# One core, attention beside a gated MLP: first-chunk key copies on ScalarE's queue, weight loads issued in unit 32, Wo's rows at unit 25

## The chip, the cores and the metric

The kernel runs on one core of a Trainium2 chip. A core has a matrix engine (TensorE, PE in the profile; its weight loads are PEld), VectorE (DVE), ScalarE (ACT), GpSimd (POOL) and SyncE (SP), which here only issues DMAs. Each engine takes its own instructions in program order and meets the others through semaphores. DMAs are issued from SyncE's and ScalarE's instruction queues and are carried out by 16 DMA engines. The metric is device time in microseconds (us) of one execution.

## What is computed

One transformer block on 2048 tokens of width 576: attention with 32 heads of 18 and a sliding window of 256, and a gated MLP of width 4608, both on the same normalised input.

```python
def reference(A_x, A_wqkv, A_wo, B_x, B_w1, B_w3, B_w2):
    # H = 32; Dh = 18; W = 256
    xn = _layernorm(A_x)
    q, k, v = split_heads(xn @ A_wqkv)
    scores = einsum("bhqd,bhkd->bhqk", q, k) * Dh ** -0.5
    mask = (i - j >= 0) & (i - j < W)
    p = softmax(where(mask, scores, -1e9))
    attn = merge_heads(p @ v) @ A_wo
    mlp = (silu(xn @ B_w1) * (xn @ B_w3)) @ B_w2
    return A_x + attn + mlp
```

## The kernel before

The program is one instruction stream for each engine, written out by Python: `add(engine, fn, r=..., w=..., j=...)` appends an instruction and notes which buffers it reads, writes or joins in writing, and the needed semaphore waits follow from that. The place of the `add` call in the Python program is the place on the engine.

The tokens are worked in four chunks `c` of 512. In a chunk, TensorE goes through 36 **units** `u` (`NF`): unit `u` makes 128 rows of the MLP's hidden layer, 9 pairs `n` of matmuls each (line 860), half of them on `xnT` (the normalised input, transposed) and half on `xnS` (the same with its two halves of partitions swapped by DMA). A unit's result goes through `unit_tanh` on ScalarE (L869) and `unit_h` on VectorE (L875, L878). Three pairs of PSUM banks take turns. Between the pairs of matmuls stand the score matmuls of attention (L682; their exponential on ScalarE is L691, masks on GpSimd L718), and now and then a block of P·V (L739). At the end of a chunk come the projections of the next chunk's Q, K and V (L496) and then the second MLP matmul with Wo (`w2_lanes`: L1036, L1045, with a part of the next chunk's scores, L756).

Four things in it are touched by the change:

- **The MLP's first weights.** A tile `w13` holds the weights of four units (fc 0 to 8 of a chunk). `load_part` (L343) issues the next part of the next tile from SyncE. Parts are `owed`: the counter is raised after certain units, and after pairs 3 and 8 of each unit `owe_part(op)` issues one, behind that matmul. The two parts of the next chunk's first tile (fc 9 counted through) were issued at the start of the projections, after `xn_swap` (L460).
- **The first chunk's last keys.** `kn` holds keys in a second layout for the groups `g` 0 to 3; its first 256 columns (`knp`) are, for chunk 1, the last 256 keys of chunk 0. `first_prev(only)` (L653) copies them out of `stage` in eight DMAs: three of 18 partitions x 4 groups x 256, three of 18 x 256 and two of 9 x 256. They were issued from SyncE in units 18 to 25, one in each. `kn` is cleared by GpSimd ahead of them, at unit 15 (L1480).
- **Wo's first rows.** Four DMAs (L1477) load `wo[0:126]` from SyncE; the rest (`wo_late`) follows in the projections. `wo` is first read in `w2_lanes` of chunk 0.
- **What stands near them on SyncE**: the transposes of the next chunk's input (`xnT<-xn`, L453), the attention outputs' moves (`oT<-od`, L817), the loads of `w2` (L379), in program order.

Of the kernel before, what the change touches and what calls it, by code (L numbers as in the profile page):

```python
# [44 lines left out]
class _Prog:  # L45
# [13 lines left out]
    def add(self, eng, fn, r=(), w=(), j=(), dma=None, after=()):  # L59
        deps = []  # L60
        for k in r:
            deps += self.bufs[k].writers
        for k in w:
            g = self.bufs.get(k)
            if g is not None:
                deps += g.ahead(eng)
        for k in j:
            g = self.bufs[k].before
            if g is not None:
                deps += g.ahead(eng)  # L70
        op = _Op(eng, fn, deps + list(after), dma)
        op.after = tuple(after)
        self.n[eng] += 1
        op.pos = self.n[eng]
        if dma is not None:
            self.dma_count[dma] = self.dma_count.get(dma, 0) + 16
            op.cnt = self.dma_count[dma]
        for k in r:
            self.bufs[k].readers.append(op)
        for k in w:  # L80
            self.bufs[k] = _Gen([op], self.bufs.get(k))
        for k in j:
            self.bufs[k].writers.append(op)
        for k in w:
            if self.bufs[k].before is not None:
                self.bufs[k].before.before = None
        self.ops.append(op)
        return op
# [76 lines left out]
def bass_parallel_sum__sliding_block__glu_gated_swiglu__prompt_kernel(  # L165
# [18 lines left out]
    NC = S // CH  # L184
# [11 lines left out]
    add = P.add  # L196

    with ExitStack() as es:
# [65 lines left out]
        def st_keys(*tiles):  # L264
            return [("sh", t) for t in tiles]
# [27 lines left out]
        def job():  # L293
            nonlocal job_ctr
            i = job_ctr % 3
            job_ctr += 1
            return JOBS[i]
# [24 lines left out]
        def w13_at(k):  # L322
            if k == 3:
                return NW13, hT[:, 18:27, :]
            s = (k if k < 3 else k - 1) % NW13
            return s, w13[s]

        owed = 0
# [4 lines left out]
        def load_part(after=(), behind=(), eng="sp"):  # L333
            nonlocal nfill
            if nfill >= len(parts_of):
                return
            k, n, a, b = parts_of[nfill]
            first = a == 0 and n == 0
            s, dst = w13_at(k)
            c0 = (k % NFC) * 512  # L340
            src = (B_w3, B_w1)[n]
            nfill += 1
            add(eng, lambda e: e.dma_start(  # L343
                dst[64 * n:64 * n + 64, a:b, :],
                src[64 * a:64 * b, c0:c0 + 512].rearrange("(kd p) f -> p kd f", p=64)),
                r=list(behind), after=after, dma=f"w13_{s}_{n}", **{"w" if first else "j": [("w13", s)]})
# [182 lines left out]
        def proj_end(later=None):  # L529
            if pend:  # L530
                c, what, banks, last = pend.pop()
                proj_part(c, what, banks, 1, last)
                proj_out(c, what, banks, later)
                return what
# [106 lines left out]
        def last_keys(g, to, of):  # L641
            if g != SPREAD:
                r0 = (g - (g > SPREAD)) * Dh
                return [(kn[96:96 + Dh, g, to], stage[r0:r0 + Dh, 8, of], [8])]
            return [(kn[96 + r:96 + r + 2 * 9 - 1:2, g, to], stage[126 + r:127 + r, :, of], range(9)) for r in range(2)]

        def first_prev(only):
            moves = [(kn[32 * h:32 * h + Dh, :, 0:W], stage[(4 + h) * Dh:(5 + h) * Dh, 0:GN, CH - W:CH], range(GN)) for h in range(3)]
            for g in range(GN):
                moves += last_keys(g, slice(0, W), slice(CH - W, CH))  # L650
            for n, (dst, src, tset) in enumerate(moves):
                if n in only:
                    add("sp", lambda e, dst=dst, src=src: e.dma_start(dst, src), r=st_keys(*tset), dma="knp",  # L653
                        **{"j" if n else "w": [("knp", g) for g in range(GN)]})

        def keep_new(g):
# [4 lines left out]
        def keep_keys(g):  # L661
            add("pool", lambda e: e.tensor_copy(
                kb4[:, g - GN, :, :].bitcast(dt.float32), kv[:, g, 2 * NB - NV:NB, :].bitcast(dt.float32)),
                r=[("k", g)], w=[("kp", g)])
# [485 lines left out]
        for p in range(2):  # L1150
            add("act", lambda e, p=p: e.dma_start(
                wvr[64 * p:64 * p + 64, :], A_wqkv[512:576, 2 * D + p * HD:2 * D + (p + 1) * HD]),
                dma="wvd", **{"j" if p else "w": ["wvd"]})
# [11 lines left out]
        for h in range(2):  # L1165
            for n in range(2):
# [3 lines left out]
                    dma=f"wqk{h}", **{"j" if n else "w": [f"wqk{h}"]})  # L1170
# [33 lines left out]
        def turn(i):  # L1204
# [6 lines left out]
            r=[("sm", 2), "eps"], w=[("sm", 3)])  # L1211
# [23 lines left out]
        for h in range(2):  # L1235
# [13 lines left out]
            for k0, k1, need, key, which in parts:  # L1249
                for n, (dst, src) in enumerate(moves[m] for m in which):  # L1250
                    dealt.append(add("pool", lambda e, dst=dst[:, k0:k1], src=src[:, k0:k1]: e.tensor_copy(dst, src),
                                     r=need + ([] if dealt else [("xnd", 1)]), **{"j" if n else "w": [key]}))
# [45 lines left out]
        for c in range(NC):  # L1298
# [93 lines left out]
            for u in range(NF):  # L1392
# [77 lines left out]
                    span_last(2, G, slice(0, 1))  # L1470
                if c == 0 and u in (5, 6):
                    span_last(2, G, (slice(1, 3), slice(3, None))[u - 5])
                if c == 0 and u == 13:
                    for t in range(4):
                        a0 = (4 + 14 * (t // 2)) * Dh
                        rows = A_wo[a0:a0 + 14 * Dh, :].rearrange("(s p d) f -> p s d f", p=2, d=Dh)[t % 2, :, :, :]
                        add("sp", lambda e, t=t, rows=rows: e.dma_start(wo[0:126, t, :], rows),  # L1477
                            dma="wo", **{"j" if t else "w": ["wo"]})
                if c == 0 and u == 15:
                    add("pool", lambda e: e.memset(kn[:, :, :].bitcast(dt.float32), 0.0),  # L1480
                        w=[(k, g) for k in ("kn", "knp") for g in range(GN)])
                if c == 0 and u == 20:
                    add("dve", lambda e: e.memset(wz[:], 0.0), w=["wz"])
                if c == 0 and 18 <= u < 26:
                    first_prev((u - 18,))
                if u in (range(27, 31) if c == 0 else range(LATE_PV + 5, LATE_PV + 12, 2)):
                    load_w2(c * 2 * NFC + 4)
                if u == 29 and c + 1 == NC:
# [3 lines left out]
            if c + 1 < NC:  # L1492
                banks = job()
                pv(c, 3, banks)
                for g in range(GN, G):
                    keep_keys(g)
                if c == 0:
                    add("pool", lambda e: e.memset(mk16[:, :, :], -1.0), w=["mkn"] + [("k", g) for g in range(GN)])
                    add("pool", lambda e: e.affine_select(
                        out=mk16[:, 0, :], in_=mk16[:, 0, :], compare_op=ALU.is_ge, fill=0.0,  # L1500
                        base=-1, pattern=[[-1, 128]], channel_multiplier=1), r=["mkn"], w=["mkn"])
                    add("pool", lambda e: e.affine_select(
                        out=mk16[:, 1, :], in_=mk16[:, 1, :], compare_op=ALU.is_ge, fill=0.0,
                        base=0, pattern=[[1, 128]], channel_multiplier=-1), r=["mkn"], w=["mkn"])
                    v0_readers = {p: list(P.bufs[("va", p)].readers) for p in range(NB)}
                for m, what in enumerate(PROJ_LATER + [None]):
                    got = proj_begin(c + 1, what) if what else proj_end()
                    if m == 0:
                        xn_swap(c + 1, ("sp", "sp"))
                        for _ in range(2):  # L1510
                            load_part()
                        if c == 0:
                            wo_late()
                        for u in sorted(side):
                            for do in side.pop(u):
                                do()
                        pv_out(banks[0], 0)
                        pv_out(banks[1], 1)
                        o_scale(0)
                    elif m == 1:  # L1520
                        o_turn(6, 0)
                        o_turn(6, 1)
                        o_scale(1)
                    elif m == 2:
                        o_turn(7, 0)
                        o_turn(7, 1)
                    if got == ("q", 2):
                        new_k(0)
                        new_k(1)
                    elif got and got[0] == "8":  # L1530
                        new_k(2)
                    if m == 6:
                        o_pack(3, "sp")
                    if 3 <= m < 7:
                        new_q(m - 3, "act")
                    owe_part(last_pe())
                i_last = (job_ctr - 1) % 3
                live = [*SC, *JOBS[(i_last + 1) % 3]]
                late_pv = w2_lanes(c, live, [*JOBS[(i_last - 1) % 3], *JOBS[i_last]])
                continue  # L1540
# [52 lines left out]
```

## Time and profile before

| | |
|---|---|
| median of 3 runs | 555.41 us (555.14 to 555.68) |
| profiled execution | 555.78 us, of which the span of instructions is 554.0 |
| TensorE clock granted | 1.00 throughout |
| TensorE busy | 548.4 us, 99% |
| VectorE, ScalarE, GpSimd busy | 66%, 53%, 22% |
| DMA | 88.12 MB, 159 GB/s on average |

A row of the profile's groups and timelines gives the line of the program, the engine, the operation, what it writes and reads (`out<-in`) and a count; a timeline row begins with the start and the duration in us, and ends with the idle time before it and what ended that. ACTq and SPq are the instruction queues of ScalarE and SyncE, in which DMA issues stand. Times are from the start of the span. The chain of work that ended last is TensorE for 96% of the span. In chunk 0 the units run from 21.1 to 103 us, in chunks 1 to 3 from 163 to 239, 299 to 375 and 434 to 510.

### The profile page before, as it was taken

To read this page: it belongs to the slowest core of one execution; us is meant where nothing else is said; L and a number is where in the kernel's file an instruction comes from. 1 tells how busy PE (TensorE), PEld (TensorE's weight loads), DVE (VectorE), ACT (ScalarE), POOL (GpSimd) and SP (SyncE) were. 2 spreads that over 40 slices of the span, in tenths; PEclk is the share of its full clock that TensorE was granted. 3 is DMA by queue.
4 is the path that set the end of the run, shared out by engine and by line. 5 is a ranking of instruction groups with operands and counts; after the bars stand their busy time and mean duration, and the time that the engine had idled before them with its cause. 6 is when DMAs were issued, how large, how long until landed. Compare 5 with 4: busy or idle time off the path is not lost.

```text
span 554.0 us, 17657 instructions
## 1 busy us (share of the span) xinstructions
PE 548.4 (99%) x7690; PEld 301.9 (54%) x7690; DVE 365.0 (66%) x745; ACT 294.0 (53%) x481; POOL 120.1 (22%) x281
## 2 busy tenths in 40 slices
PE   8999999999999999999999999999999999999998
PEld 4455444465564444456556445446555644545776
DVE  6566898845748888674664888866466686676211
ACT  6457775268735554526882655443787355554000
POOL 5413653300003332210001342320000222221000
DMA  9997989549999998965979999767697999881552
GB/s 243 208 193 141 205 159 183 137 97 176 156 163 202 187 197 134 155 130 116 155 136 190 197 198 189 147 101 156 120 160 125 196 196 165 168 167 61 139 151 64
DMA packets 166070, 88.12 MB, mean 159 GB/s; under 512 B 101546, under 2 KB 163754, under 8 KB 165994
## 3 DMA queue, kind: packets, MB, share of 16 engines
q1 hardware_dynamic: 164874, 85.42, 82.3%
q10 hardware_dynamic: 1120, 1.59, 1.0%
q8 instruction: 60, 0.98, 0.8%
q14 instruction: 16, 0.13, 0.1%
HBM read 71.30 MB, written 2.36 MB: 133 GB/s over the span
## 4 chain that ended last, share of the span: by engine, by line
PE 96%; DMA 2%; SPq 1%; issue 0%; ACT 0%; DVE 0%
PE ps L860 50%; PE ps L1036 17%; PE ps L496 7%; PE ps L932 6%; PE ps L682 4%; PE ps L1086 2%; PE ps L739 2%; PE ps L1045 2%; DMA xnS<-xnT 2%; PE ps L791 2%; PE ps L756 1%; PE ps L1160 1%; PE ps L939 1%; SPq L343 1%; PE ps L1096 0%
## 5 line engine op out<-in xcount | busy, mean ns | idle before, releaser
L860 PE MATMUL ps<-xnT,w 64*128 64x512 bf16 x1400 | 177.5, 376 | 0.8 <-issue 0.8
L860 PE MATMUL ps<-xnS,w 64*128 64x512 bf16 x1120 | 148.6, 376 | 0.7 <-DMA xnS<-xnT 0.7
L875 DVE SCALAR_TENSOR_TENSOR gs<-thb,ps 128x512 bf16<-128x512 bf16 x144 | 98.6, 684 | 67.2 <-ACT thb L869 66.7
L869 ACT ACTIVATE thb<-ps 128x512 bf16<-128x512 f32 x144 | 85.7, 595 | 59.8 <-PE ps L860 58.6
L1036 PE MATMUL ps<-hT,w 32*128 32x512 bf16 x1728 | 107.0, 374 | 0.0
L860 PEld LDWEIGHTS ps<-xnT,w 64*128 64x128 bf16 x1400 | 67.2, 94 | 72.5 <-issue 1.0
L878 DVE SCALAR_TENSOR_TENSOR hT<-gs,ps 128x512 bf16<-128x512 bf16 x144 | 98.9, 687 | 5.0
L860 PEld LDWEIGHTS ps<-xnS,w 64*128 64x128 bf16 x1120 | 53.7, 94 | 58.1 <-DMA xnS<-xnT 1.1
L1036 PEld LDWEIGHTS ps<-hT,w 32*128 32x128 bf16 x1728 | 57.5, 92 | 30.2 <-issue 1.4
L763 ACT ACTIVATE pt<-ps 128x512 bf16<-128x512 f32 x120 | 65.1, 595 | 7.7 <-PE ps L756 7.5
L691 ACT ACTIVATE pt<-ps 128x1024 bf16<-128x1024 f32 (+1 forms) x46 | 46.2, 1004 | 43.0 <-PE ps L682 42.9
L756 PE MATMUL ps<-qv,kn 18*128 18x384 bf16 (+2 forms) x288 | 54.5, 267 | 0.0
L806 POOL TENSOR_TENSOR oq<-uq,rden 128x288 bf16<-128x288 f32 x15 | 10.1, 673 | 198.6 <-DVE rden L805 198.6
L718 POOL TENSOR_TENSOR pt<-pt,mk 128x128 int32<-128x128 int32 (+1 forms) x82 | 33.1, 424 | 69.4 <-ACT pt L691 69.4
L771 DVE TENSOR_TENSOR pt<-pt,kv 128x256 int32<-128x256 int32 x96 | 31.4, 371 | 24.8 <-ACT pt L763 24.2
L496 PE MATMUL ps<-xnT,wp 64*128 64x512 bf16 (+1 forms) x360 | 38.0, 355 | 0.0
L932 PE MATMUL ps<-w,hT 128*128 128x288 bf16 (+1 forms) x292 | 36.9, 284 | 0.0
L691 ACT ACTIVATE hT<-ps 128x1024 bf16<-128x1024 f32 (+1 forms) x20 | 20.0, 1002 | 31.5 <-PE ps L682 31.4
L756 PEld LDWEIGHTS ps<-qv,kn 18*128 18x128 bf16 x288 | 26.5, 93 | 13.8 <-DVE uq L800 0.8
L932 PEld LDWEIGHTS ps<-w,hT 128*128 128x128 bf16 x292 | 28.2, 98 | 7.3 <-issue 0.2
L682 PE MATMUL ps<-qv,kv 64*128 64x320 bf16 (+4 forms) x336 | 31.7, 258 | 0.0
L813 DVE STREAM_TRANSPOSE od<-oq 128x256 bf16<-128x256 bf16 x64 | 25.1, 424 | 6.3 <-POOL oq L806 6.3
(128 smaller groups left out, 523.4 us busy)
## 6 DMA issues: line engine op xcount, KB each, us to landing
w<-in_B_w_dram SPq DMA_DIRECT2D x60, 576.0 KB, 7.8
w<-in_B_w_dram SPq DMA_DIRECT2D x72, 288.0 KB, 4.4
w<-in_B_w_dram SPq DMA_DIRECT2D x12, 192.0 KB, 6.8
xp<-in_A_x_dram SPq DMA_DIRECT2D x4, 576.0 KB, 5.4
xnS<-xnT SPq DMA_DIRECT2D x8, 256.0 KB, 4.4
xp<-in_A_x_dram SPq DMA_DIRECT2D x14, 144.0 KB, 4.2
w<-in_B_w_dram SPq DMA_DIRECT2D x6, 320.0 KB, 4.8
oT<-od SPq DMA_DIRECT2D x52, 36.0 KB
```

Of the source, the lines that this page charges most:

```text
L496: op = add("pe", lambda e, out_=out_, st=st, mv=mv, n=n, r0=r0, first=first: e.matmul(out_, st, mv, start=first, stop=(part == 1 and n == ...
L682: add("pe", lambda e, r0=r0, out_=out_, kb=kb, q0=q0, nb=nb: e.matmul(out_, kb4[r0:r0 + 64, g - GN, kb + NV - NB, :] if kb < 0 else kv[r0: ...
L691: add("act", lambda e: e.activation(pt_slot(sl)[:, 0:w, :], PS[:, SC[0]:SC[1] + 1, 0:w].rearrange("p r q -> p q r"), ACT.Exp, scale=scale) ...
L718: add("pool", lambda e, vb=vb, mm=mm: e.tensor_tensor(vb, vb, mm, ALU.mult), r=(key if n == 0 else []) + ["mk"], **{"w" if n == 0 else "j" ...
L756: add("pe", lambda e: e.matmul(PS[:, b, c0:c0 + nb * 128], kn[32 * a:32 * a + Dh, g, W + 128 * jb:W + 128 * jb + 128], qv[32 * a:32 * a + ...
L763: add("act", lambda e: e.activation(head_of(sl, p), PS[:, b, :], ACT.Exp, scale=scale), r=[("ps", b)], **{"j" if p else "w": pt_keys(sl)})
L860: op = add("pe", lambda e, n=n, r0=r0, r=r, k=k, src=src: e.matmul(PS[:, b0 + r, :], wt[r0:r0 + 64, k, fl * 128:(fl + 1) * 128], src, star ...
L869: add("act", lambda e: e.activation(th[i][:], PS[:, bg, :], ACT.Tanh, scale=0.5), r=[("ps", bg)], w=[("th", i)])
L875: add("dve", lambda e: e.scalar_tensor_tensor(out=gs[i][:], in0=th[i][:], scalar=1.0, in1=PS[:, bg, :], op0=ALU.add, op1=ALU.mult), r=[("t ...
L878: add("dve", lambda e: e.scalar_tensor_tensor(out=hT[:, u, :], in0=gs[i][:], scalar=0.5, in1=PS[:, bu, :], op0=ALU.mult, op1=ALU.mult), r= ...
L932: add("pe", lambda e: e.matmul(bank, hT[:, f, tt * 128:(tt + 1) * 128], w2[sl][:, k, n0:n1], start=first, stop=(c + 1 == NC and half == 1 ...
L1036: add("pe", lambda e, b=b, rows=rows, wt=wt, fl=fl, k=k, a=a, first=first: e.matmul(PS[:, b, :], wt[rows, fl, :], hT[rows, k, :], start=fi ...
```

## The change

The key copies are issued by ScalarE, two after each of units 1 to 4, and the clearing of `kn` moves to unit 0. Wo's first rows are issued at unit 25 instead of 13. Two more parts are owed after unit 31 in chunks 0 to 2, so that they are issued behind pairs 3 and 8 of unit 32, and the two calls at the start of the projections go.

```diff
@@ first_prev @@
-                    add("sp", lambda e, dst=dst, src=src: e.dma_start(dst, src), r=st_keys(*tset), dma="knp",
+                    add("act", lambda e, dst=dst, src=src: e.dma_start(dst, src), r=st_keys(*tset), dma="knp",
                         **{"j" if n else "w": [("knp", g) for g in range(GN)]})
@@ after each unit @@
-                if c == 0 and u == 13:
+                if c == 0 and u == 25:
                     for t in range(4):
...
                         add("sp", lambda e, t=t, rows=rows: e.dma_start(wo[0:126, t, :], rows),
                             dma="wo", **{"j" if t else "w": ["wo"]})
-                if c == 0 and u == 15:
+                if c == 0 and u == 0:
                     add("pool", lambda e: e.memset(kn[:, :, :].bitcast(dt.float32), 0.0),
                         w=[(k, g) for k in ("kn", "knp") for g in range(GN)])
...
-                if c == 0 and 18 <= u < 26:
-                    first_prev((u - 18,))
+                if c == 0 and 1 <= u < 5:
+                    first_prev((2 * u - 2, 2 * u - 1))
+                if u == 31 and c + 1 < NC:
+                    owed += 2
@@ projections @@
                     if m == 0:
                         xn_swap(c + 1, ("sp", "sp"))
-                        for _ in range(2):
-                            load_part()
                         if c == 0:
                             wo_late()
```

The instructions on TensorE and on VectorE keep their order. On ScalarE, in the first units of chunk 0 (`thb` is the tanh of a unit, `hT<-ps` the first exponential of the scores), the order changes so:

```order
 L1286 ACTIVATE thb<-neghalf 128x1
-L869 ACTIVATE thb<-ps 128x512 x6
+L869 ACTIVATE thb<-ps 128x512 x2
+L653 DMA kn<-stage 18x4x256 x2
+L869 ACTIVATE thb<-ps 128x512
+L653 DMA kn<-stage 18x4x256
+L653 DMA kn<-stage 18x256
+L869 ACTIVATE thb<-ps 128x512
+L653 DMA kn<-stage 18x256 x2
+L869 ACTIVATE thb<-ps 128x512
+L653 DMA kn<-stage 9x1x256 x2
+L869 ACTIVATE thb<-ps 128x512
```

Four pairs of DMA issues stand between the tanhs of units 1 to 5. On SyncE, between units 12 and 24 of chunk 0, the queue held before, around the load of fc 8 (`w_1`):

```order
L817 DMA oT<-od 16x512
L653 DMA kn<-stage 18x256
L817 DMA oT<-od 16x512
L653 DMA kn<-stage 18x256
L817 DMA oT<-od 2x1024
L653 DMA kn<-stage 18x256
L343 DMA w_1<-in_B_w_dram 64x9x512 x2
L817 DMA oT<-od 2x1024
L453 DMA_TRANSPOSE xnT<-xn 128x5x128
L653 DMA kn<-stage 9x1x256
L817 DMA oT<-oT 64x512
```

and holds now, in the same place and on to the loads of `w2` (L379) and the next chunk's first tile (`w_2`):

```order
L343 DMA w_1<-in_B_w_dram 64x9x512 x2
L817 DMA oT<-od 2x1024
L453 DMA_TRANSPOSE xnT<-xn 128x5x128
L817 DMA oT<-oT 64x512
L1477 DMA wo<-in_A_wo_dram 126x1x576 x4
L453 DMA_TRANSPOSE xnT<-xn 128x5x128
L379 DMA w_0<-in_B_w_dram 128x9x128
L379 DMA w_1<-in_B_w_dram 128x9x128
L379 DMA w_2<-in_B_w_dram 128x9x128
L817 DMA oT<-od 18x1024 x4
L379 DMA w_3<-in_B_w_dram 128x9x128
L343 DMA w_2<-in_B_w_dram 64x9x512 x2
```

The key copies are gone from between the moves of `oT`, Wo's rows stand behind the load of fc 8 instead of ahead of all of this, and the load of the next chunk's first tile (last row) stands ahead of the swap of `xnS`.

## The prediction

> **What bounds the kernel.** I read the page first. TensorE is busy in 99% of a span of 554.0 us, so a change can win little: only what TensorE stands still. Next, TensorE's own waits, which name all of it behind the start.
>
> ```profile
> PE 548.4 (99%) x7690; PEld 301.9 (54%) x7690; DVE 365.0 (66%) x745; ACT 294.0 (53%) x481; POOL 120.1 (22%) x281
> q8 instruction: 60, 0.98, 0.8%
> PE ps L860 <- issue: 0.8, 1, 0.8
> PE ps L860 <- DMA xnS<-xnT: 0.7, 1, 0.7
> PE ps L739 <- issue: 0.4, 1, 0.4
> ```
>
> The columns of a wait are total us, times, longest. After the first matmul there are three standstills: one on the first swapped copy `xnS` (0.7, ahead of everything that the change touches), and two that the profile calls "issue": no semaphore explains them. The timeline of TensorE places these two:
>
> ```profile
> 54.30 0.22 PE L739 MATMUL ps<-hT,va 64*20 64x128 bf16 x2
> 54.87 0.23 PE L739 MATMUL ps<-hT,va 64*20 64x128 bf16 x2 [0.35 <-issue]
> ...
> 90.12 0.38 PE L682 MATMUL ps<-qv,kv 64*128 64x320 bf16 x6
> 91.31 0.82 PE L860 MATMUL ps<-xnT,w 64*128 64x512 bf16 x6 [0.81 <-issue]
> ...
> 54.70:90.90 36.20, 35.63 (x508) 18.09 (x507) 32.81 (x67) 25.58 (x34) 19.83 (x46) 1.00 1.09 180
> ```
>
> The last row is a window between the two (its counts are TensorE's matmuls, then weight loads): 508 + 507 = 1,015 instructions, beside a few that only wait. The page has 60 packets of instructions, 0.98 MB, for 2 x 7,690 matmuls and weight loads: 256 instructions to a packet. So the two standstills lie about four packets (1,024) apart, at the same place of a packet. I read both as **TensorE waiting for its next packet of instructions**, which comes by DMA. Queue rows of small windows show when those packets came:
>
> ```profile
> q1 hardware_dynamic: 1495, 1.21, 103.7%
> ...
> q8 instruction: 1, 0.02, 8.2%
> ...
> q1 hardware_dynamic: 1205, 1.00, 119.4%
> ...
> q8 instruction: 1, 0.02, 41.9%
> ```
>
> The first row is all that 46 to 52 us has: SyncE's queue alone, and no instructions; the second is in 52 to 53. The third is all of 83.5 to 88.4; the fourth is in 88.4 to 88.6. Each packet runs when a stretch of SyncE's loads at some 200 GB/s (1.21 MB in 6 us, 1.00 in 4.9) is through, and TensorE resumes 2 to 3 us later (54.87, 91.31). That a packet comes late because the weight loads are ahead of it is inferred from this order.
>
> **The change part by part.** The order on TensorE and on VectorE is the same before and after: no arithmetic is added or removed. All of it is in DMA issues and one clearing.
>
> *The eight copies into `kn`, on ScalarE.* What an issue costs, in rows of one line each (ns: shortest, median, longest):
>
> ```profile
> L653 SPq DMA_DIRECT2D kn<-stage x8: 745/801/890, 68.9 to 85.6; - x8
> L625 ACTq DMA_DIRECT2D qv<-stage x12: 717/722/1005, 111.8 to 386.6; - x12
> L585 ACTq DMA_DIRECT2D qv<-stage x2: 762/1047/1332, 16.4 to 17.7; - x2
> ...
> 112.58 0.41 ACT L547 ACTIVATE va<-ps 128x288 bf16<-128x288 f32 x1 [0.97 <-PE ps L496]
> 112.66 0.72 ACTq L625 DMA_DIRECT2D qv<-stage  x1
> 112.89 0.57 ACT L547 ACTIVATE va<-ps 64x144 bf16<-64x144 f32 x2
> ...
> 26.07 0.60 ACT L869 ACTIVATE thb<-ps 128x512 bf16<-128x512 f32 x1 [1.34 <-PE ps L860]
> 28.02 0.60 ACT L869 ACTIVATE thb<-ps 128x512 bf16<-128x512 f32 x1 [1.35 <-PE ps L860]
> ...
> 33.84 0.60 ACT L869 ACTIVATE thb<-ps 128x512 bf16<-128x512 f32 x1 [1.34 <-PE ps L860]
> 35.36 1.02 ACT L691 ACTIVATE hT<-ps 128x1024 bf16<-128x1024 f32 x1 [0.92 <-PE ps L682]
> 36.65 0.40 PE L682 MATMUL ps<-qv,kv 64*128 64x320 bf16 x6
> ```
>
> A pair at the median for these very copies is 2 x 0.80 = 1.60 us. It need not be added to the 0.60 of a tanh: at 112.6 the two activations at 112.89 stand ahead of the issue in the program and run during it, so the queue goes on issuing while the engine works. Behind each pair waits the next tanh, ready 1.95 us after the last one (26.07, 28.02): 1.60 fits, cost 0. At the dearest row (2 x 1.332 = 2.66) each pair would be 0.72 late; after four pairs the tanh due at 33.84 starts at 36.7, the exponential due at 35.36 at 37.3, 1.9 late, and the score matmul at 36.65, which reuses its bank, has 36.65 - (35.36 + 1.02) = 0.27 of room: 1.7 us. At the cheapest (0.717) nothing is won, as ScalarE loses no work. Range 0 to +1.7; I take 0, from the rows of the same copies.
>
> *The clearing of `kn` on GpSimd* goes ahead of them:
>
> ```profile
> 20.10 0.95 POOL L1279 MEMSET kb<- 128x1024 f32 x1
> 36.47 0.73 POOL L718 TENSOR_TENSOR hT<-hT,mk 128x128 int32<-128x128 int32 x2 [15.41 <-ACT hT L691]
> 61.69 1.38 POOL L1480 MEMSET kn<- 128x1536 f32 x1
> ```
>
> It takes 1.38 and now starts at 21.05, in 15.41 idle us, and is done at 22.4, before the first copy at 26.1. Cost 0; at 61.69 it is gone from an engine that is off the path.
>
> *What SyncE is rid of.* Eight copies at 0.80 are 6.4 us of issue between 68.9 and 86.3, and Wo's rows:
>
> ```profile
> 31.75 10.46 SPq L585 DMA_DIRECT2D kv<-stage  x3
> 44.52 2.67 SPq L343 DMA_DIRECT2D w<-in_B_w_dram  x4
> 57.88 4.14 SPq L1477 DMA_DIRECT2D wo<-in_A_wo_dram  x4
> 80.61 1.41 SPq L343 DMA_DIRECT2D w<-in_B_w_dram  x2
> 74.79 1.24 PE L860 MATMUL ps<-xnT,w 64*128 64x512 bf16 x10
> wo<-in_A_wo_dram SPq DMA_DIRECT2D x4, 141.8 KB
> ```
>
> The weights of fc 8 are issued at 80.61 and run until about 88, ahead of the late packet. They may go once TensorE is in unit 24, whose first matmuls are in the row at 74.79, so at about 76; until 80.61 they stood behind Wo's four issues (4.14) and six copies (4.8). Now they go some 4.5 us earlier and are through by about 84. Wo's rows come right behind them instead: 4 x 141.8 KB at 202 GB/s (1.21 MB in the 6 us of the first queue row) is 2.8 us, so through by 87 if the packet waits for all of that. Either way it is at least 1 us earlier than 88.5, and **the second standstill goes**: 0.81 by the idle row; by the starts 91.31 - 90.12 = 1.19, less the 0.22 that six such score matmuls take elsewhere (rows below), 0.97. Its bound on the other side: if Wo's rows are added and the weights aren't earlier, it grows by 2.8.
>
> The first standstill hangs on the four loads at 44.52, the last of which is the nearest to 52. The `kn` copies bring 147 KB (three of 18 x 4 x 256 elements of 2 B, three of 18 x 256, two of 9 x 256) into 26 to 34 us, 0.8 us at the 178 GB/s that I take from the stretch 21 to 53 (its row is below), on rings that SyncE is waiting for: three issues take 10.46. SyncE then comes to the loads up to 0.8 us later, so up to one load more (256 KB, 1.3 us at 202) is behind the packet instead of ahead: **0.35 by the idle row to 0.57 by the starts** (54.87 - 54.30) is won. At the other end the packet is 0.8 later and as much is lost. I take the gain, since the standstill needs only 0.57.
>
> ```profile
> 21.00:53.00 32.00, 31.32 (x324) 17.01 (x322) 19.72 (x29) 19.86 (x28) 7.24 (x19) 1.00 0.94 178
> ...
> 65.35 0.38 PE L682 MATMUL ps<-qv,kv 64*128 64x320 bf16 x6
> 65.57 0.60 PE L860 MATMUL ps<-xnS,w 64*128 64x512 bf16 x4
> ```
>
> *The early loads in unit 32* of each chunk are two issues, behind nothing that TensorE waits for: no wait of TensorE after 91.31 is in the list above. The slot is free since unit 27 and the tile is wanted by the next chunk; the swap of `xnS` behind them waits for unit 35 anyway. Cost and gain 0; a packet of instructions near them may shift by some tenths either way.
>
> Sum, against the profiled execution's 555.78 (span 554.0 and 1.8 around it): -0.81 to -0.97, -0.35 to -0.57: 554.2 to 554.6. The median of the runs shown is 555.41, so the profile's execution holds 0.37 more than usual, perhaps in these very standstills; they can only go to zero, so the end is the same. I take 554.5.
>
> Two pages of the Trainium skill speak against this. Runtime: NRT & Kernel Launch, Instruction fetch mechanics, says that TensorE's instructions stream in blocks of 16 KiB, ahead of their use, and that crossing a block is mostly hidden. By that rule the two rows are no fetch and the time stays at 555.4. The block agrees with 0.98 MB in 60 packets; "hidden" doesn't fit 0.35 and 0.81 at the same place of a block. DMA: Bandwidth & Descriptors, Queues, rings and completion order, says that a DMA engine takes turns between rings packet by packet; by that an instruction packet would never stand behind six microseconds of SyncE's loads, and moving loads would move no standstill. The rows of 46 to 53 and 83.5 to 88.6 speak against it.
>
> **The rivals.** *Nothing moves.* The standstills aren't due to the loads, or one goes and another packet becomes late, since the same bytes must pass and only move by some microseconds: 554.9 to 555.9. For it: DMA moves 178 GB/s from 21 to 53 us and 180 from 54.7 to 90.9, and Wo's 567 KB now lie just before the second packet. Against it: the order of the rows above.
>
> *ScalarE is held behind SyncE: slower.* The last pair is issued at about 32 to 33.5, and SyncE's issue that begins at 31.75 takes 10.46 us for three, where such a copy costs under one: it stands on full rings. If ScalarE's issue stands too until SyncE gets on (one of the two long ones, to about 37), the tanh due at 33.84 and the exponential due at 35.36 go at 37.1 and 37.7, 2.3 late, and after 0.27 of room TensorE stands 2.0 us. It decides from the point where a pair takes over 1.95 us. Time 556.5 to 557.5, by whether the standstills go. For it: 1.332 for an issue at 16.4 beside SyncE's. Against it: the twelve issues of L625 keep a median of 0.722 in stretches in which SyncE issues too.
>
> *A later packet: slower.* One standstill grows by 1 to 2.8 us behind Wo's rows: 556 to 558.
>
> **How the numbers follow.** Forecast, both standstills gone or nearly: 0.45, 554.1 to 554.9. Nothing moves: 0.36. ScalarE held: 0.11. A later packet: 0.08. About 0.2%, 1.1 us, is what a measurement of this kernel tells from no change: faster is below 554.3, slower above 556.5. Faster comes from the low end of the forecast, below 554.3, 0.17; slower from the two last, 0.13; the rest, 0.70, is no change. The range leaves out the last rivals and a sliver below: 553.9 to 556.6.
>
> **What would show it.** Right: no "issue" row among TensorE's waits, or smaller ones at 54 and 91; tanh starts still 1.95 apart between 24 and 36; pairs of issues of about 1.6 us on ScalarE's queue; the load of 80.61 at about 76. Wrong: a tanh in that stretch that starts later than its matmuls end, scores that wait for ScalarE, an "issue" row elsewhere, or the two where they were though the loads moved.

## The result and the profile after

| kernel | median, us | lowest to highest | runs |
|---|---|---|---|
| before | 555.84 | 554.90 to 558.62 | 20 |
| changed | 554.85 | 553.60 to 555.85 | 20 |

The ratio is 0.9977, with a 95% interval of 0.9967 to 0.9986: about 1.3 us less (0.8 to 1.8 by the interval). A second comparison, beside other kernels further down, gave 0.9979 (0.9954 to 1.0003). The profiled execution took 554.85 us with a span of 553.1, where the one before took 555.78 with 554.0.

All waits of TensorE in the changed kernel (total us, times, longest):

```profile
PE ps L1160 <- DVE oq L1154: 1.2, 1, 1.2
PE ps L496 <- ACT xnT L447: 0.5, 1, 0.5
PE ps L496 <- POOL mk L1270: 0.4, 1, 0.4
PE ps L739 <- issue: 0.3, 1, 0.3
PE ps L496 <- DMA wv<-in_A_wqkv_dram: 0.3, 1, 0.3
```

The "issue" row of L860, 0.8 us before, is gone. That of L739 is still there with 0.3 in place of 0.4. The others lie in the first 21 us, ahead of everything that the change touches. The wait for `xnS` is absent here, but also from profiles below whose kernels are untouched at that place (Wo's rows alone, the early loads alone), so its loss is no work of the change.

TensorE's timeline at the two places (start, duration, operation, idle time before it):

```profile
54.13 0.22 PE L739 MATMUL ps<-hT,va 64*20 64x128 bf16 x2
54.64 0.23 PE L739 MATMUL ps<-hT,va 64*20 64x128 bf16 x2 [0.30 <-issue]
...
89.89 0.38 PE L682 MATMUL ps<-qv,kv 64*128 64x320 bf16 x6
90.11 0.81 PE L860 MATMUL ps<-xnT,w 64*128 64x512 bf16 x6
```

From 89.89 to 90.11 is 0.22 us, where before it was 1.19: 0.97 won. From 54.13 to 54.64 is 0.51, where it was 0.57: 0.06 won. That nothing else moved much is read from the starts of the same matmuls in both profiles: the changed kernel is 0.17 ahead at the first place (54.30 to 54.13), 0.23 behind it (90.12 to 89.89), 1.20 after the second (91.31 to 90.11), and 0.9 at the end (554.0 to 553.1). The 0.3 between is lost at 342 us, in a block of P·V of chunk 2:

```profile
340.91 0.38 PE L860 MATMUL ps<-xnT,w 64*128 64x512 bf16 x2
...
342.81 0.40 PE L682 MATMUL ps<-qv,kv 64*128 64x320 bf16 x6
```

That is 1.90 us for a stretch that took 1.63 before (342.11 to 343.74).

ScalarE and its queue, in the units in which it now issues the copies:

```profile
25.90 0.60 ACT L869 ACTIVATE thb<-ps 128x512 bf16<-128x512 f32 x1 [1.34 <-PE ps L860]
25.91 1.68 ACTq L653 DMA_DIRECT2D kn<-stage  x2
27.84 0.60 ACT L869 ACTIVATE thb<-ps 128x512 bf16<-128x512 f32 x1 [1.35 <-PE ps L860]
27.85 1.61 ACTq L653 DMA_DIRECT2D kn<-stage  x2
...
33.67 0.60 ACT L869 ACTIVATE thb<-ps 128x512 bf16<-128x512 f32 x1 [1.34 <-PE ps L860]
35.18 1.02 ACT L691 ACTIVATE hT<-ps 128x1024 bf16<-128x1024 f32 x1 [0.92 <-PE ps L682]
```

The issue of each pair begins with the tanh ahead of it and takes 1.5 to 1.7 us, beyond the tanh's 0.60; the tanhs still come 1.94 apart, each released by TensorE. The exponential starts at 35.18 (35.36 before).

SyncE's queue:

```profile
46.22 2.67 SPq L343 DMA_DIRECT2D w<-in_B_w_dram  x4
...
75.84 1.91 SPq L343 DMA_DIRECT2D w<-in_B_w_dram  x2
...
80.80 3.32 SPq L1477 DMA_DIRECT2D wo<-in_A_wo_dram  x4
```

The weights of fc 8 go at 75.84 (80.61 before), Wo's rows behind them at 80.80, and fc 4's four loads 1.7 us later than before (44.52). The instruction packets, in small windows of the queues (packets, MB, share of 16 engines):

```profile
q1 hardware_dynamic: 1172, 1.14, 95.0%
...
q8 instruction: 1, 0.02, 16.9%
...
q8 instruction: 1, 0.02, 20.4%
```

The first row is 46.2 to 51.7 us, with no instructions; the second is 51.7 to 52.2; the third is 85.2 to 85.6. The fourth packet, counted from the program's start, begins at 51.79 (52.07 before), the eighth at 85.29 in place of 88.51.

### The profile page after: what moved, and what is told of

It is laid out like the page before. It is cut to its first block, busy times and chain, and to the rows that moved or that the text cites. A ratio compares the mean times of both kernels' runs of the same rounds, so it can differ in the third digit from the quotient of the medians.

```text
span 553.1 us, 17657 instructions
## 1 busy us (share of the span) xinstructions
PE 548.0 (99%) x7690; PEld 301.7 (55%) x7690; DVE 365.2 (66%) x745; ACT 294.0 (53%) x481; POOL 120.0 (22%) x281
## 3 DMA queue, kind: packets, MB, share of 16 engines
q1 hardware_dynamic: 164514, 85.27, 82.2%
## 4 chain that ended last, share of the span: by engine, by line
PE 97%; DMA 1%; SPq 1%; POOL 0%; issue 0%; DVE 0%
PE ps L860 51%; PE ps L1036 17%; PE ps L496 8%; PE ps L932 6%; PE ps L682 4%; PE ps L739 2%; PE ps L1086 2%; PE ps L1045 2%; PE ps L791 2%; PE ps L756 1%; DMA pt<-in_A_wqkv_dram 1%; PE ps L939 1%; SPq L1168 0%; PE ps L1096 0%; SPq L1172 0%
## 5 line engine op out<-in xcount | busy, mean ns | idle before, releaser
L860 PE MATMUL ps<-xnT,w 64*128 64x512 bf16 x1400 | 177.5, 376 | 0.0
L860 PE MATMUL ps<-xnS,w 64*128 64x512 bf16 x1120 | 148.6, 376 | 0.0
L869 ACT ACTIVATE thb<-ps 128x512 bf16<-128x512 f32 x144 | 85.6, 595 | 58.9 <-PE ps L860 57.7
L860 PEld LDWEIGHTS ps<-xnT,w 64*128 64x128 bf16 x1400 | 67.2, 94 | 71.6
L860 PEld LDWEIGHTS ps<-xnS,w 64*128 64x128 bf16 x1120 | 53.7, 94 | 57.3
L691 ACT ACTIVATE pt<-ps 128x1024 bf16<-128x1024 f32 (+1 forms) x46 | 46.2, 1005 | 42.2 <-PE ps L682 42.2
```

What stands on the lines that cost most here:

```text
L691: add("act", lambda e: e.activation(pt_slot(sl)[:, 0:w, :], PS[:, SC[0]:SC[1] + 1, 0:w].rearrange("p r q -> p q r"), ACT.Exp, scale=scale) ...
L860: op = add("pe", lambda e, n=n, r0=r0, r=r, k=k, src=src: e.matmul(PS[:, b0 + r, :], wt[r0:r0 + 64, k, fl * 128:(fl + 1) * 128], src, star ...
L869: add("act", lambda e: e.activation(th[i][:], PS[:, bg, :], ACT.Tanh, scale=0.5), r=[("ps", bg)], w=[("th", i)])
```

## The experiments

Three questions were open: are the standstills really waits for packets of 256 instructions; does the weight traffic delay these packets; and which part of the change holds the gain. Ratios are to the kernel before, run on the same chip beside each kernel.

**Where a standstill opens.** From the changed kernel, whose order on TensorE is that of before: 32 and then 128 instructions (short matmuls and their weight loads) are added to the warm-up, which moves every later instruction within its packet:

```diff
-        warm(4, *[CH] * 10)
+        warm(4, *[CH] * 9, *[64] * 17)
```

The second kernel has `*[CH] * 5, *[64] * 69`; a warm-up matmul of width 64 uses 32 columns of weights.

> The changed kernel with the warm-up of TensorE cut otherwise: 9 matmuls of 512 columns and 17 of 64 in place of 10 of 512, so 32 instructions (16 matmuls and their weight loads) more ahead of everything. Theory (a standstill comes at a fixed count of instructions, 256 to a packet): each packet is needed 32 instructions earlier in the program and also asked for 1.7 us earlier, ahead of the block of P.V; the standstill in the first P.V block (0.3 to 0.5) goes, no other above 0.3 comes: 0.2 to 0.6 us faster than the changed kernel. Rival (the standstill belongs to the P.V block): it stays where it is, and the time with it.

> As the kernel before this one, with 5 matmuls of 512 columns and 69 of 64: 128 instructions more. Theory: the joint block of P.V (256 instructions in 1.9 us, at 82 to 84 us) now lies whole between the asking for a packet and the need for it, so a standstill of 2.5 to 4 us just behind it, at 84 to 86 us, and some of 0.3 to 0.6 near 60 and 210; 2.5 to 4.5 us slower than the changed kernel (about 1 us of it may come from a longer warm-up). Rival (standstills belong to places in the program): nothing new at 84 to 86, time within 1 us.

Measured: 32 gave 1.0008 (0.9986 to 1.0031), 128 gave 1.0126 (1.0085 to 1.0166). Windows from the start of the program into a standstill count the instructions ahead of it (matmuls behind "PE busy", weight loads behind "PEld busy"). The kernel before:

```profile
0.00:54.60 54.60, 52.43 (x600) 28.04 (x601) 34.38 (x67) 33.41 (x55) 21.40 (x51) 1.00 0.94 197
0.00:90.80 90.80, 88.06 (x1108) 46.13 (x1108) 67.20 (x133) 58.90 (x89) 41.23 (x97) 1.00 1.00 190
```

The kernel with 32 more, its window and its standstill:

```profile
0.00:89.00 89.00, 86.69 (x1108) 46.54 (x1108) 66.06 (x131) 58.20 (x87) 40.49 (x95) 1.00 1.04 192
```

```profile
87.91 0.38 PE L860 MATMUL ps<-xnS,w 64*128 64x512 bf16 x2
90.36 0.61 PE L860 MATMUL ps<-xnS,w 64*128 64x512 bf16 x4 [2.06 <-issue]
```

The kernel with 128 more:

```profile
0.00:85.00 85.00, 81.74 (x1109) 52.19 (x1109) 62.11 (x123) 54.31 (x82) 38.76 (x91) 1.00 1.01 195
```

```profile
88.02 0.27 PE L739 MATMUL ps<-w,va 64*20 64x128 bf16 x1 [4.51 <-issue]
```

The place in the program changes (a unit's matmuls behind scores, the middle of a unit's matmuls, the P·V), but the count stays: 2,216, 2,216 and 2,218 instructions, and 1,201 for the first standstill. The windows leave out what only waits or signals; with those counted in the trace, the instruction that comes late is number 1,218 and 2,242, that is 4 and 8 times 256, plus 194. On these instructions TensorE waits for no semaphore in the trace. With 32 more the first standstill is gone, as expected, but the eighth packet comes at 87.76 and costs 2.06, so the forecast of a faster kernel missed. With 128 more the standstill is longer than forecast, and so is the time. A standstill is tied to a count of instructions and to a packet, then. Neither shift makes the kernel faster.

**The copies alone**, from the kernel before, with the clearing:

```diff
-                    add("sp", lambda e, dst=dst, src=src: e.dma_start(dst, src), r=st_keys(*tset), dma="knp",
+                    add("act", lambda e, dst=dst, src=src: e.dma_start(dst, src), r=st_keys(*tset), dma="knp",
-                if c == 0 and 18 <= u < 26:
-                    first_prev((u - 18,))
+                if c == 0 and 1 <= u < 5:
+                    first_prev((2 * u - 2, 2 * u - 1))
```

> The kernel before with the key copies on ScalarE and the clearing at unit 0 alone. Theory (the second standstill is a packet of instructions behind the fc 8 weights): six copies, 4.8 us of SyncE's time, are gone from ahead of the fc 8 load, so it is issued at 76 to 78 us instead of 80.6, its packet of instructions runs at 86 to 87 instead of 88.5, the second standstill falls from 0.81 to 0.3 or less, the first stays at 0.3 to 0.4: 0.5 to 1.0 us faster than before. Rival (it takes Wo's move to clear the way): the fc 8 load at about 80, both standstills as before, time within 0.2 us of before.

Measured: 1.0017 (1.0001 to 1.0034). The load of fc 8 did go at 75.59, and the eighth packet came at 87.94. But the waits have a new row, and so has the timeline:

```profile
PE ps L739 <- issue: 0.8, 1, 0.8
...
PE ps L860 <- issue: 0.2, 1, 0.2
```

```profile
82.94 0.31 PE L739 MATMUL ps<-w,va 64*20 64x320 bf16 x3
84.01 0.31 PE L739 MATMUL ps<-w,va 64*20 64x320 bf16 x1 [0.75 <-issue]
```

The matmul at 84.01 is instruction 1,986, 7 times 256 plus 194: the seventh packet now comes at 81.16, behind the load that was moved to 75.59. The largest standstill went one packet ahead, and the eighth stays late. The theory that this part alone wins 0.5 to 1 us falls.

**Wo's rows alone**, from the kernel before: `if c == 0 and u == 13:` becomes `u == 25:`.

> The kernel before with Wo's first rows at unit 25 alone. Theory: 4.1 us of SyncE's time are gone from ahead of the fc 8 load, the copies stay: issued at 76.5 to 78, the packet at 86 to 87.5, the second standstill 0.3 or less unless Wo's rows now hold the packet up; 0.5 to 1.0 us faster. Rival (Wo's rows just ahead of the packet delay it as much as the weights did): packet at 88 or later, second standstill 0.8 or more, no gain or a loss of up to 1 us.

Measured: 0.9997 (0.9976 to 1.0017). The eighth packet comes at 87.34, so that the second standstill is gone. The first has 0.5 here, and another transfer is late:

```profile
PE ps L756 <- DMA qv<-stage: 1.1, 1, 1.1
PE ps L739 <- issue: 0.5, 1, 0.5
```

The first row, at 119.9, names its transfer: the next chunk's first scores wait for the fourth copy of Q, issued at 113.79 and landed at 119.7.

**The early loads alone**, from the kernel before (the two `load_part()` behind the swap are out, `owed += 2` at unit 31 is in).

> The kernel before with the next chunk's first weights issued in unit 32 alone. Theory: nothing that TensorE waits for is touched: both standstills stay (0.35 and 0.8), time within 0.2 us of before. Rival (the early loads free the projections or the joint part): projections shorter, 0.3 us or more gained after 104 us of the span.

Measured: 0.9994 (0.9981 to 1.0007). The second standstill stays with 0.8, as expected. The first, expected to stay as well, is absent: the fourth packet begins at 47.17, though the program is that of before up to unit 31. The largest new row has nothing to do with the edit, which acts behind it:

```profile
PE ps L739 <- DVE hT L878: 1.4, 1, 1.4
...
PE ps L860 <- issue: 0.8, 1, 0.8
```

VectorE had waited for a transpose of `xn` at 82.2: a third kind of transfer that is in time in most profiles and late in this one.

**One part left out.** The changed kernel with Wo's rows back at unit 13, then without the early loads, then with the copies back on SyncE in units 18 to 25 (each the reverse of a diff above).

> The changed kernel with Wo's first rows back at unit 13. Theory: the copies' going alone lets the fc 8 load go at 76, so the second standstill stays gone and the time is that of the changed kernel within 0.2 us (1.0 us below before). Rival (Wo's move is needed): the second standstill back at 0.5 to 0.8, time 0.2 us or less below before.

> The changed kernel with the next chunk's first weights issued at the start of the projections again (copies on ScalarE and Wo at unit 25 stay). Theory (all of the gain is made before 92 us, by the copies and Wo's rows together): second standstill gone, time that of the changed kernel within 0.2 us. Rival (the early loads count too: behind fc 9's weights the fourth Q copy of the projections lands 5 to 6 us after its issue, as with Wo's move alone, where TensorE waited 1.1 us for it): a wait of the joint part's scores for Q or K of 0.5 to 1.2 us, and 0.3 to 1.0 us slower than the changed kernel.

> The changed kernel with the key copies back on SyncE in units 18 to 25 (Wo at unit 25 and the early loads stay). Theory: Wo's going alone is half of it: fc 8's load at 78 to 79.5 us, the packet at 86.5 to 88, second standstill 0 to 0.5; 0.2 to 0.6 us slower than the changed kernel. Rival (copies and Wo's rows each suffice): as the changed kernel within 0.2 us.

Measured: without Wo's move 1.0017 (1.0001 to 1.0033), without the early loads 0.9991 (0.9971 to 1.0012), without the copies' move 1.0005 (0.9981 to 1.003). Without Wo's move, the waits and the timeline show the first standstill and one a packet ahead of the second:

```profile
PE ps L739 <- issue: 1.5, 2, 0.9
```

```profile
54.18 0.23 PE L739 MATMUL ps<-hT,va 64*20 64x128 bf16 x2 [0.57 <-issue]
...
84.44 0.31 PE L739 MATMUL ps<-w,va 64*20 64x320 bf16 x1 [0.89 <-issue]
```

The second row is instruction 1,986 again. The theory that the copies' going is enough falls here too. Without the copies' move the second standstill has 2.3 us, at instruction 2,242, where 0 to 0.5 was expected. The load of fc 8 (78.74) and the packet (87.22) came as forecast, but TensorE resumes 3.5 us after the packet's end, where it is 1.3 to 1.6 in all other standstills; that wasn't explained. So the gain needs Wo's move: both kernels with the copies on ScalarE and Wo's rows still at unit 13 are slower than the changed kernel, beyond the intervals. That it needs the copies' move as well is likely, but not shown: the intervals without it (0.9976 to 1.0017, 0.9981 to 1.003) overlap that of the changed kernel.

The early loads were tried once more, on one chip beside the changed kernel:

> The changed kernel once more, beside the others on this chip. Theory (a small gain made of several transfers that come up to a microsecond late in some executions and in time in others): a median 0.5 to 2 us below that of before, a profile whose standstills, if it has any, open at instruction 194 of a block of 256, though not with the lengths of the first profile. Rival (the 1.3 us of the first comparison was chance): within 0.3 us of before.

> The changed kernel without the early loads in units 32 and 33, once more, beside the changed kernel on this chip. If the early loads are worth nothing, as predicted: within 0.4 us of the changed kernel run beside it. If they are worth what the two first comparisons suggest (0.9977 against 0.9991): 0.5 to 1 us slower than the changed kernel.

Measured: the changed kernel 0.9979 (0.9954 to 1.0003), without the early loads 0.9968 (0.9942 to 0.9994), medians 554.93 and 554.82. The early loads are worth nothing that can be measured. The two profiles show how the standstills come and go between executions. That of the changed kernel has one at instruction 9,922, 38 times 256 plus 194, at 342 us:

```profile
PE ps L739 <- issue: 0.2, 1, 0.2
```

and the one without the early loads has one at instruction 1,986, and none at 54:

```profile
82.58 0.31 PE L739 MATMUL ps<-w,va 64*20 64x320 bf16 x3
83.41 0.31 PE L739 MATMUL ps<-w,va 64*20 64x320 bf16 x1 [0.52 <-issue]
```

**What delays a packet.** From the kernel before, with the bytes of two loads cut and their issues kept:

```diff
             nfill += 1
+            if k in (4, 8):
+                b = a + 1
             add(eng, lambda e: e.dma_start(
```

> The kernel before, with the loads of fc 4's and fc 8's gate and up weights cut to one block of 64 rows out of every five or nine (2/9 and 1/9 of their bytes), so that SyncE issues the same instructions in the same order and only the traffic is gone; the results of these two fc are not the reference's. Theory (the standstills are waits for an instruction packet that the weight traffic delays): packet 4, which begins at 52.07 us in the profile before, begins by 49, and packet 8 (88.51) by 86; the standstill of 0.35 at 54.5 and that of 0.81 at 90.5 are both gone, and no new one opens; a median of 0.6 to 1.3 us less than before. Rival (the packet is asked for late, whatever else moves): packets 4 and 8 begin within 0.7 us of their old times and both standstills stay; within 0.3 us of before. Rival (the instruction queue is late because of the 1,152-byte and 128-byte packets of the transposes and copies): packet 8 stays late, packet 4 too.

Measured: 0.9965 (0.994 to 0.9991), a median 1.7 us below, more than forecast. No "issue" row is left among TensorE's waits. The timeline at both places (lines are two further down in this kernel):

```profile
54.23 0.31 PE L741 MATMUL ps<-w,va 64*20 64x128 bf16 x3
54.48 0.37 PE L684 MATMUL ps<-qv,kv 64*128 64x320 bf16 x4
...
89.70 0.38 PE L684 MATMUL ps<-qv,kv 64*128 64x320 bf16 x6
89.92 0.81 PE L862 MATMUL ps<-xnT,w 64*128 64x512 bf16 x6
```

The queues of two windows, 46.3 to 47.6 and 84.0 to 85.2 us:

```profile
q8 instruction: 1, 0.02, 4.2%
...
q8 instruction: 1, 0.02, 5.0%
```

The fourth packet begins at 47.39 in place of 52.07, the eighth at 84.72 in place of 88.51. With the same issues on SyncE and only the bytes gone, both packets are in time, and the median agrees.

For the eighth packet the other profiles bear this out: the traffic delays it, not a late request. From the start of instruction 1,955, which is 287 ahead of the one that comes late, to the packet's begin it takes 5.0 and 6.6 us where all loads there are as before (before, the early loads alone), 4.2 to 5.5 in the four kernels with one of the two moves, 1.6 to 3.0 in four profiles with both (the changed kernel and that without the early loads, two each), and 1.7 with the bytes cut. The 5.4 with 32 instructions more, where the loads are those of the changed kernel, isn't explained. For the fourth packet it isn't shown: the early loads alone had it at 47.17 with all bytes in place, so one profile with 47.39 can be chance.

**The loads behind the packet.** The changed kernel, with the last keys' copies ahead of fc 4's loads:

```diff
-                if c == 0 and u in (5, 6):
-                    span_last(2, G, (slice(1, 3), slice(3, None))[u - 5])
+                if c == 0 and u == 3:
+                    span_last(2, G, slice(1, None))
```

> The changed kernel with the six copies of the last keys moved on SyncE from behind to ahead of fc 4's four weight loads, which so start some 5 us later (46.2 to about 51). Theory (packet 4, asked for at about 46.1, waits for the weight loads that are issued at that time): packet 4 begins by 49 in place of 51.79, the standstill of 0.30 at 54.35 is gone, and fc 4's second half lands at about 59 to 60 where TensorE wants it from 57.2 to 58.5, so that a wait for the weights of 0.5 to 2 us takes its place; 0.3 to 1.5 us slower than the changed kernel. Rival (it waits for anything that SyncE issues): packet 4 stays at 51 to 52 and the standstill stays as well as the wait for the weights.

Measured: 1.0049 (1.002 to 1.0078), and a median 3.3 us above that of before and 4.6 above the changed kernel's. SyncE's queue, and TensorE's timeline:

```profile
42.36 6.57 SPq L614 DMA_DIRECT2D kv<-stage  x7
...
49.97 2.67 SPq L343 DMA_DIRECT2D w<-in_B_w_dram  x4
```

```profile
56.10 0.38 PE L860 MATMUL ps<-xnT,hT 64*128 64x512 bf16 x2
58.57 1.04 PE L860 MATMUL ps<-xnT,w 64*128 64x512 bf16 x8 [2.09 <-issue]
```

The packet begins at 47.08 and the first standstill is gone; in its place TensorE stands 2.09 us until fc 4's last load lands at 58.48. So the rival that a packet waits for anything that SyncE issues didn't hold in this profile: seven copies from 42.36 on didn't keep it back. The price was set too low: the profiled execution (556.02) is the lowest of twelve. For the others only time and clock are on record: the mean granted clock is 1.00 in the two fastest (556.02 and 556.81) and 0.994 or 0.997 in the other ten (558.45 to 561.87). Over some 558 us that is worth 1.7 to 3.3 us, an estimate; how long their standstills were wasn't seen. An "issue" row need not be a packet, either: this one ends 0.1 us after a load, and the weight load at its end waits for a semaphore in the trace.

## Why the prediction was right, and where not

- **What bounds the kernel:** right. The two standstills are waits for packets, by their count of instructions, and the weight traffic makes the second late, by the cut loads and the other profiles; for the first this is not shown. Of the two rules weighed against this, that of Runtime: NRT & Kernel Launch (Instruction fetch mechanics, in the Trainium skill), that crossing a block is mostly hidden, holds for most of the 60 packets; the exceptions here cost 0.2 to 4.5 us each. That of DMA: Bandwidth & Descriptors (Queues, rings and completion order, also in the Trainium skill), turns between rings packet by packet, doesn't account for the 3.8 us between 84.72 and 88.51 for the eighth packet without and with the bytes of the loads.
- **The copies on ScalarE at no cost:** right. Pairs of 1.5 to 1.7 us in 1.94. The rival that ScalarE stands behind SyncE's full rings wasn't put to the test: SyncE's three long issues began at 33.30 and took 10.64, and ScalarE's last pair ended at 31.73 + 1.58 = 33.31.
- **The clearing at no cost:** right; it stands at 20.7 us and no copy waits for it.
- **The second standstill goes, 0.81 to 0.97:** right, 0.97 by the starts, and it is absent from the four profiles of the changed kernel and of that without the early loads. The load of fc 8 went at 75.84, as worked out (about 76). The reason was incomplete. An earlier load isn't enough, as the copies alone show: it then lies before the seventh packet, which has as little room, and the eighth still came at 87.94. There the loads of `w2` went at 84.43, ahead of that packet, and in the changed kernel at 85.76, behind it (85.29); that this decides wasn't tested. In the changed kernel the seventh has 0.2 us of room, worked out from its end (81.88), the 1.47 that TensorE takes to resume, and the matmul that needs it (83.55).
- **The first standstill goes, 0.35 to 0.57:** wrong; 0.06. The step that failed is that loads issued up to 0.8 us later would lie behind the packet instead of ahead of it. They came 1.7 us later, and the packet only 0.28 earlier. Nor need the 1.7 be the copies' work: in the four profiles with the copies on SyncE and all bytes in place the loads went at 44.1 to 45.9. The profiles show no such order: in ten of them, before and changed included, the loads were issued between 44.1 and 46.2, and the packet began anywhere from 47.2 to 52.1, not later where they were earlier. Where the bytes were cut or the loads went at 49.97 it began at 47.4 and 47.1, but 47.2 is among the ten as well. So the time at which a load is issued doesn't say how late this packet is; what decides that stays open.
- **The early loads at no cost and no gain:** right within the scatter.
- **The sum:** 554.2 to 554.6 against 554.85 for the profiled execution. The second standstill paid 0.97, the first 0.06 of 0.35 to 0.57, the start 0.17, and 0.27 was lost at packet 38. The median fell by 1.0, from 555.84 to 554.85, as far as from the 555.41 of the first three runs to the forecast of 554.5 (0.9); the ratio of 0.9977 lies just past the 0.2% that the text set for "faster", to which it gave 0.17. That the total came out as forecast is in part luck: the two standstills were to give the profiled execution 1.16 to 1.54 and gave 1.03, the 0.17 of the start is no work of the change, and the range (553.9 to 556.6) would have held no change as well. The rival that one standstill goes and another packet becomes late is what the copies alone did; with Wo's rows alone it was a copy of Q that came late. The whole change only just avoids it.

## What to carry to other kernels

Where TensorE is busy in 99% of the span, look at its idle rows by the count of instructions ahead of them: rows at the same place of every 256, on instructions that wait for no semaphore, were late instructions here, and large loads in flight when the next packet is asked for are the first suspects. Cut the bytes of such a load to test it, before anything is moved, and compare more than one profile. A transfer that is moved lands before the next packet, so the room of the neighbours must be worked out as well; and with several transfers that come within a microsecond of their need, single profiles differ by more than the edit, so that only a comparison of many executions tells its worth.

## What the runs showed of the hardware

There is little time to fetch a packet where instructions are short. At the earliest, packets begin in these profiles when TensorE is some 290 instructions ahead of the first one that the packet brings. That is 7 to 15 us in the units, but two across the P·V: with 128 more instructions the eighth was needed 2.0 us after it could be asked for (worked out from the start of instruction 1,955 and the last matmul ahead of 2,242), and most packets take 0.9 to 1.4 us plus the 1.3 to 1.6 until TensorE resumes. By these sizes it would be late there by 0.2 to 1.0 us without any other traffic, an estimate that no run shows; with Wo's rows issued from 80.07 on it began 4.1 us after instruction 1,955.

A long standstill costs more than itself. In that kernel the windows around it show, in the third column from the right, the granted clock:

```profile
82.00:84.00 2.00, 1.51 (x127) 1.28 (x109) 1.69 (x4) 0.00 (x0) 0.00 (x0) 1.00 1.16 188
84.00:88.00 4.00, 0.00 (x0) 0.00 (x0) 0.72 (x3) 0.00 (x0) 0.67 (x1) 0.75 1.59 171
88.00:90.00 2.00, 1.98 (x13) 0.92 (x15) 0.72 (x1) 0.92 (x1) 0.18 (x1) 0.50 0.65 122
90.00:92.00 2.00, 2.00 (x14) 0.62 (x12) 1.24 (x2) 0.60 (x1) 0.55 (x2) 0.50 0.73 141
92.00:95.00 3.00, 3.00 (x32) 1.50 (x30) 1.64 (x5) 1.99 (x3) 1.09 (x2) 0.87 1.29 216
```

After 4.51 us without a matmul TensorE goes on at half speed until about 93 us. Against the changed kernel this stretch lost 7.0 us, 4.6 in the standstill and 2.4 in what came after, which is most of what the 128 instructions cost where 2.5 to 4.5 was expected. The standstills of up to 2.3 us left the clock at 1.00. The Trainium skill, TensorE: Matmul & The Clock Gate, Part 1: The HAM clock gate, says that an idle window of about 3.4 us halves the clock until a busy one has passed. The trace agrees in the halving, and its half-speed stretch of 6.8 us (86.0 to 92.8) is as long as two such windows; but the clock fell 2.5 us after the last matmul (83.5), sooner than a whole idle window.
